# ScalarE takes two copies ahead of a square: a recurrence with a mixture of experts on one core

## The chip, the cores and the metric

The kernel runs on one core of a Trainium2 chip. Its five engines each work through a queue of their own in order: TensorE (PE, with its weight loads as PEld), VectorE (DVE), ScalarE (ACT), GpSimd (POOL) and SyncE (SP, which issues most transfers). The metric is the device time of one execution in microseconds, as the median of several runs. A profiled execution has its own time; its span runs from the first to the last instruction.

## The reference

Per batch and head, a 48 by 48 state decays and takes in one outer product per token; the result goes through a mixture of eight experts with one expert per token.

```python
for t in range(S):                                   # 4 batches, 8 heads, 768 tokens, 48 wide
    cur = np.einsum('bhd,bhe->bhde', u[None] * kt, vt)
    y[:, :, t] = np.einsum('bhd,bhde->bhe', rt, state + cur)
    state = w[None, :, :, None] * state + np.einsum('bhd,bhe->bhde', kt, vt)
...
logits = x @ w_gate + modality_bias[modality_id]     # x: 3072 x 384, 8 experts
e_idx = np.argmax(logits, axis=1)
gate_w = probs[np.arange(N), e_idx]
out[mask] = gate_w[mask, None] * (np.maximum(x[mask] @ w1[e], 0.0) @ w2[e])
```

## The kernel before

The first part works through 24 **units**: 6 chunks of 128 tokens by 4 batches, the batches innermost. A unit's result `x` (128 tokens by 384) is made in one PSUM bank `py`; what its tokens add to the state, and the eight numbers `d` per token that carry the `u` term, are made in a bank `pst`, of which there is one only (`ps_s` has one buffer): the matmuls of the next unit's `pst` can start when all readers of this one are done. There are two `py` banks, so `py` of unit i waits for the last reader of unit i-2.

The order on every engine is the order of the code: `run` is a hand-written schedule, and nothing reorders it. Step i of its loop works on several units at once:

- PE: turns f16 rows of unit i-2 (`raised`, tile `pxT`, units 6 to 11), turns keys of unit i+2 (`keys_turned`, `pkT`), scores of unit i+1 (`scores`, `psc`), then `values(i)`: `py` (lines 475 and 482), `pst` (491 and 496) and `bonus` (411), which leaves the eight columns of `d` of unit i+1 in `pst`.
- `token(i-1)`: DVE adds `dv` to `py` (504), ACT squares the sum for its norm (519), in place for the later scaling. `taken(i)`: DVE copies the eight columns `d` out of PSUM (419). `settled_state(i-1)` (units 4 to 13) or `state(i-1)` (units 0 to 3): ACT copies the new state out of `pst` in two halves (542, 534); from unit 14 on `state` is an add on DVE.
- `own(i)`: `dv = d v`, head by head on ACT (431); of units 9 to 13 (`SHARED`) GpSimd makes the second half in one instruction (427), at the end of its step's work.
- `factor`, `high`, `low`: two small DVE instructions make a power of two from the norm (314, 316), ACT writes the scaled f16 row (552) and DVE the f16 remainder (556). `raised` turns both on PE in the next step; `flipped` copies them out on ACT (580).
- GpSimd: `rk` for `bonus` (389), `rc` (364) three units ahead, `kt` (371) two ahead, and `send` (688), an indirect transfer of finished rows to DRAM.
- SP issues the loads; `pace` makes it wait for `d` of unit i (and for the norm's factor) before the next ones.

A group of 3 or 4 units is routed together (`logits`, `choose`, `count`, `place`): chains of small DVE instructions on 8 to 32 columns, one of which `fill()` slips in at each call. Their tables lie partly in a PSUM bank `pr`, partly in SBUF (`xinv`, `zs`, `pos`). `settle` (planned at step 8) and `ahead` make the numbers for jobs that run beside the units: with step 13 the first expert's weights are ready, and eight 128-row jobs (`s_up`, `s_high`, `s_low`, `s_down`) stand among the later units. Their weights are loaded in twelve pieces, normed on ACT (961, `norm`, steps 7 to 12) and split into f16 halves `whi` (ACT, 992) and `wlo` (DVE, 997); three `wlo` of step 13 are what the first job's `s_down` waits for. From about 200 us on a loop of expert jobs fills PE.

Of the kernel before, what the change touches and what calls it, by code (L numbers as in the profile page):

```python
# [9 lines left out]
F32 = mybir.dt.float32  # L10
# [5 lines left out]
ALU = mybir.AluOpType  # L16
# [31 lines left out]
TURNED = range(1, 15)  # L48
RAISED = range(6, 12)
OWNED = range(17, 24)  # L50

NE = 9
EARLY = 3
# [12 lines left out]
class _Kernel:  # L66
# [346 lines left out]
    def taken(self, i):  # L413
        u = self.ctx_[i]
        u["d"] = self.a.tile([P, H], F32, tag="d", name=f"d{i}", bufs=4)
        if i in OWNED:
            self.nc.vector.reduce_sum(u["d"], u["rk"].rearrange("p (h e) -> p h e", e=D), axis=AX.X)
            return
        self.nc.vector.tensor_copy(u["d"], u["pd"])  # L419

    def own(self, i, q):
        nc, u = self.nc, self.ctx_[i]
        if q == 0:
            u["dv"] = self.a.tile([P, DM], F32, tag="dv", name=f"dv{i}")
        if q and i in SHARED:
            half = lambda t: t[:, DM // 2 :].rearrange("p (h e) -> p h e", e=D)
            nc.gpsimd.tensor_mul(half(u["dv"]), half(u["v"]), u["d"][:, H // 2 :].unsqueeze(2).to_broadcast([P, H // 2, D]))
            return
        for h in range(q * H // 2, (q + 1) * H // 2):
            sl = slice(h * D, (h + 1) * D)  # L430
            nc.scalar.activation(u["dv"][:, sl], u["v"][:, sl], AF.Copy, scale=u["d"][:, h : h + 1])  # L431
# [160 lines left out]
    def choose(self, u):  # L592

        nc, a, n = self.nc, self.a, u["n"]
        lg, lo = u["lg"], u["lo"]
        gb = lambda ap: ap.unsqueeze(1).to_broadcast([P, n, E])
        eb = lambda ap: ap.unsqueeze(2).to_broadcast([P, n, E])
        new = lambda t, w=E, dt=F32: (a.tile([P, B, E], dt, tag=t, name=f"{t}{lo}")[:, :n, :] if w > 1 else a.tile([P, B], dt, tag=t, name=f"{t}{lo}")[:, :n])

        xinv = a.tile([P, B, 2], F32, tag="xinv", name=f"xinv{lo}")[:, :n, 0]  # L600
        nc.vector.tensor_scalar(xinv.bitcast(I32), u["sx"][:, :n].bitcast(I32), -1.0, float(254 << 23), ALU.mult, ALU.add)
        yield
        L = u["pr"][:, 320 : 320 + n * E].rearrange("p (g e) -> p g e", g=n)
        nc.vector.reduce_sum(L, lg.rearrange("p g w e -> p g e w"), axis=AX.X)
        yield
        nc.vector.scalar_tensor_tensor(L, L, self.wginv, eb(xinv), ALU.mult, ALU.mult)
        yield
        nc.vector.tensor_add(L, L, self.lb[:, lo : lo + n, :])
        yield
        mx = new("mx", 1)  # L610
        nc.vector.reduce_max(mx, L, axis=AX.X)
        yield
        bank = lambda c, w=E: u["pr"][:, c : c + n * w].rearrange("p (g w) -> p g w", g=n)
        d = bank(384)
        nc.vector.tensor_sub(d, L, eb(mx))
        yield
        er = bank(416)
        nc.vector.scalar_tensor_tensor(er, d, 0.0, gb(self.rev), ALU.is_equal, ALU.mult)
        ex = new("ex")
        nc.scalar.activation(ex, d, AF.Exp)  # L620
        yield
        mr = new("mr", 1)
        nc.vector.reduce_max(mr, er, axis=AX.X)
        yield
        u["oh"] = new("oh", dt=F16)
        nc.vector.tensor_tensor(u["oh"], er, eb(mr), ALU.is_equal)
        yield "oh"
        zs = new("zs", 1)
        nc.vector.reduce_sum(zs, ex, axis=AX.X)
        yield  # L630
        nc.vector.scalar_tensor_tensor(zs, zs, 1e-9, u["sx"][:, :n], ALU.add, ALU.mult)
        yield
        nc.vector.reciprocal(u["row"][:, :n, 2 * DM : 2 * DM + 2].bitcast(F32).rearrange("p b o -> p (b o)"), zs)
        yield
# [13 lines left out]
    def place(self, u):  # L648
# [6 lines left out]
        yield  # L655
        nc.vector.tensor_mul(v, v, u["oh"])
        yield
        pos = a.tile([P, B], F32, tag="pos", name=f"pos{lo}")[:, :n]
        nc.vector.reduce_sum(pos, v, axis=AX.X)
        yield  # L660
        u["posi"] = a.tile([P, B], I32, tag="posi", name=f"posi{lo}", bufs=3)
# [108 lines left out]
    def settle(self):  # L770

        nc, c = self.nc, self.c
        eid = self.eid0
        nc.vector.tensor_scalar_mul(self.ctl[:, E : 2 * E], eid, float(CAP))
        yield
        self.row0f = c.tile([1, 1], F32, name="row0f")
        nc.vector.tensor_scalar_mul(self.row0f, eid[:, 0:1], float(CAP))
        yield
        self.row0m = c.tile([1, 1], F32, name="row0m")
        yield  # L780
        nc.vector.tensor_scalar_add(self.row0m, self.row0f, -float(E * CAP + P))
        yield

    def ahead(self, ks, u=None):
# [364 lines left out]
    def run(self):  # L1149
# [99 lines left out]
        for i in range(NU - 1):  # L1249
# [13 lines left out]
            if down is not None:  # L1263
                self.s_high(down, 1)
                self.s_down(down, 0)
            if i == O + 5:
                self.settled_state(i - 1)
            self.token(i - 1) if i else None
            if ups.get(i - 2) is not None:
                self.s_take(ups[i - 2])  # L1270
            if i and i - 1 == self.grp["lo"]:
                groups[i - 1] = self.grp
            fill()
            each(i, self.taken) if i else None
            if i != O + 5:
                each(i - 1, self.settled_state)
            if i - 2 in RAISED:
                self.flipped(i - 2)
            if 0 < i < NU - 5:
# [1 line left out]
                each(i + 5, self.turned)  # L1281
            half(2 * (i - O) + 4)
            for j in range(2):
                each(i - 1, lambda i: self.state(i, j))
                fill()
            if down is not None:
                self.s_low(down, 1)
# [272 lines left out]
```

## Time and profile before

| | |
|---|---|
| median of 3 runs | 342.07 us (338.2 to 344.01) |
| profiled execution: time | 343.19 us |
| profiled execution: span | 341.3 us, granted TensorE clock 0.997 |
| busy: PE, PEld | 322.7 us (95%), 262.8 us (77%) |
| busy: DVE, ACT, POOL | 213.3 us (63%), 180.1 us (53%), 160.5 us (47%) |
| chain that ended last | 12 pieces, the last 3 us of the span |

The chain that ended last reaches back over the end alone, so it says nothing of the units. PE's busy share is the number to take apart by stretches: what is left of PE's time, and who ends its waits, is in the rows below.

### The profile page before, as it was taken

Reading aid. Unit: us, or ns where it says so; the run is one execution under the profiler, and the core shown is the slowest. Engines: PE = TensorE matmul, PEld = TensorE weight load, DVE = VectorE, ACT = ScalarE, POOL = GpSimd, SP = SyncE. Lnnn points to the kernel's source line nnn. Section 1 sums busy time; section 2 is a strip of 40 time slices with the busy share of each in tenths; the row PEclk is TensorE's granted clock in tenths of the full one; section 3 lists DMA queues with packets and bytes.
Section 4 is the critical chain, followed back from the end, with each engine's and each line's share of the span. In section 5 each row is a group of like instructions: output and inputs, shape, how many; then the busy total and the mean of one; then the engine's idle time right before and its main releaser. Section 6 shows DMA issues by size and latency. Waiting matters only on the chain. (4 is left out here: it accounts for less than half of the span.)

```text
span 341.3 us, 15249 instructions
## 1 busy us (share of the span) xinstructions
PE 322.7 (95%) x5459; PEld 262.8 (77%) x5459; DVE 213.3 (63%) x745; ACT 180.1 (53%) x482; POOL 160.5 (47%) x237
## 2 busy tenths in 40 slices
PE   7999998889899999899999999999999999999992
PEld 3788897778778888687887778886888887777771
DVE  7868987489997997587758732268322332334950
ACT  7787788578766568367532222265222224553820
POOL 8978779688739786526268411112122111211211
PEclk9999999999999999999999999999999999999998
DMA  6766999667659999995345632217611121112110
GB/s 187 237 165 161 169 250 301 181 224 169 182 139 234 195 281 285 235 131 147 71 130 175 190 96 65 47 46 249 195 46 46 47 69 23 46 52 64 37 46 5
DMA packets 58013, 47.93 MB, mean 140 GB/s; under 512 B 42344, under 2 KB 50807, under 8 KB 57712
## 3 DMA queue, kind: packets, MB, share of 16 engines
q1 hardware_dynamic: 54768, 37.85, 46.9%
q0 software_dynamic: 3200, 9.47, 7.7%
q8 instruction: 30, 0.49, 0.6%
q14 instruction: 15, 0.12, 0.1%
HBM read 27.21 MB, written 11.83 MB: 114 GB/s over the span
## 5 line engine op out<-in xcount | busy, mean ns | idle before, releaser
L1051 PEld LDWEIGHTS <-whi 128*128 128x128 f16 x1248 | 72.4, 98 | 3.8 <-issue 0.9
L1060 DVE SCALAR_TENSOR_TENSOR hl<-phb,hh 128x256 f16<-128x256 f32 (+1 forms) x48 | 24.4, 508 | 68.3 <-ACTq L1491 68.3
L1114 PEld LDWEIGHTS <-hh 128*128 128x128 f16 x416 | 39.1, 98 | 27.6 <-issue 2.2
L1051 PE MATMUL phb<-mxT,whi 128*128 128x128 f16 x768 | 50.8, 219 | 0.0
L431 ACT ACTIVATE dv<-kv,d 128x48 f32<-128x48 f32 x172 | 43.1, 325 | 0.4 <-DVE d L419 0.2
L1055 ACT ACTIVATE hh<-phb 128x256 f16<-128x256 f32 (+1 forms) x48 | 21.5, 455 | 32.6 <-PE phb L1051 21.9
L1051 PEld LDWEIGHTS <-wlo 128*128 128x128 f16 x624 | 37.7, 98 | 0.0
L1020 POOL TENSOR_TENSOR seenb<-otb,putb 128x1 int32<-128x1 int32 x16 | 4.4, 275 | 64.0 <-ACTq L1491 51.9
L451 DVE TENSOR_TENSOR at<-psc,mask 128x512 f32<-128x512 f32 x48 | 31.9, 682 | 1.9 <-PE psc L445 1.8
L364 POOL TENSOR_TENSOR rc<-ud,powr 112x512 f32<-112x512 f32 (+1 forms) x25 | 31.0, 1243 | 0.7 <-DMA ud<-in_pd 0.5
L1114 PEld LDWEIGHTS <-hl 128*128 128x128 f16 x208 | 19.4, 98 | 15.3 <-issue 2.5
L1011 ACT ACTIVATE otb<-po,fac 128x384 f32<-128x384 f32 x16 | 9.3, 580 | 39.5 <-PE phb L1051 36.1
L688 POOL DMA_INDIRECT rows<-row,posi x24 | 25.0, 1042 | 10.8 <-DVE base L664 3.1
L445 PE MATMUL psc<-rc,kc 64*64 64x128 f32 (+1 forms) x768 | 27.1, 276 | 2.3 <-issue 1.5
L1051 PE MATMUL phb<-mxT,wlo 128*128 128x128 f16 x384 | 29.3, 219 | 0.0
L1114 PE MATMUL po<-whi,hl 128*128 128x384 f16 x136 | 28.0, 326 | 1.2 <-PEq L1556 0.7
L1114 PE MATMUL po<-whi,hh 128*128 128x384 f16 x136 | 27.7, 326 | 0.5 <-ACT hh L1055 0.4
L1114 PE MATMUL po<-wlo,hh 128*128 128x384 f16 x136 | 27.6, 326 | 0.0
L1051 PE MATMUL phs<-mxT,whi 128*128 128x128 f16 x432 | 27.2, 219 | 0.0
L445 PEld LDWEIGHTS psc<-rc,kc 64*64 64x64 f32 (+1 forms) x768 | 20.9, 132 | 7.9 <-issue 4.2
L482 PE MATMUL py<-kv,at 128*64 128x48 f32 x768 | 26.5, 221 | 0.0
L997 DVE SCALAR_TENSOR_TENSOR wlo<-raw,ws,whi 128x1024 f16<-128x1024 f32 (+1 forms) x20 | 25.0, 1277 | 1.4 <-issue 0.6
(287 smaller groups left out, 636.0 us busy)
## 6 DMA issues: line engine op xcount, KB each, us to landing
kv<-in_pt SPq DMA_DIRECT2D x21, 384.0 KB
ud<-in_pd SPq DMA_DIRECT2D x10, 384.0 KB
raw<-in_w SPq DMA_DIRECT2D x12, 256.0 KB
raw<-in_w SPq DMA_DIRECT2D x6, 512.0 KB
raw<-in_w SPq DMA_DIRECT2D x2, 1536.0 KB, 6.3
ud<-in_pd SPq DMA_DIRECT2D x14, 192.0 KB
rows<-pad SPq DMA_DIRECT2D x10, 193.0 KB
rt<-in_pt SPq DMA_DIRECT2D x7, 192.0 KB
```

The source lines that it names most:

```text
L364: nc.gpsimd.tensor_mul(u["rc"][:TOP, s], u["rT"][:TOP, s], self.powr[:TOP, s])
L431: nc.scalar.activation(u["dv"][:, sl], u["v"][:, sl], AF.Copy, scale=u["d"][:, h : h + 1])
L445: nc.tensor.matmul(u["ps"][j][s, pr * P : (pr + 1) * P], u["kc"][r, pr, s], u["rc"][r, pr, :], start=True, stop=True)
L451: nc.vector.tensor_mul(u["at"][:, j * NPR : (j + 1) * NPR, :], u["ps"][j].rearrange("p (q t) -> p q t", q=NPR), self.mask.unsqueeze(1).to_ ...
L482: nc.tensor.matmul(py[t, sl], u["at"][:, j * NPR + pr, t], u["v"][:, sl], start=c == h == 0, stop=h == H - 1, skip_group_check=True)
L688: i = nc.gpsimd.indirect_dma_start(out=self.rows, out_offset=bass.IndirectOffsetOnAxis(ap=u["posi"][:, b : b + 1], axis=0), in_=u["row"][: ...
L997: self.nc.vector.scalar_tensor_tensor(self.wlo[:, sl], self.raw[:, sl], sc, self.whi[:, sl], ALU.mult, ALU.subtract)
L1011: self.nc.scalar.activation(ot, po[:, :DM], AF.Copy, scale=gf[:, t : t + 1])
L1051: self.nc.tensor.matmul(ph[:, q * P : (q + 1) * P], w[:, c0 : c0 + P], self.xT[:, xq, t * P : (t + 1) * P], start=i == q == 0, stop=i == l ...
L1055: self.nc.scalar.activation(self.hh[:, f0 : f0 + fb, t * P : (t + 1) * P], p3, AF.Relu)
L1060: self.nc.vector.scalar_tensor_tensor(self.hl[:, f0 : f0 + fb, r], p3, 0.0, self.hh[:, f0 : f0 + fb, r], ALU.max, ALU.subtract)
L1114: self.nc.tensor.matmul(po[:, :DM], h[:, f, t * P : (t + 1) * P], w[:, c0 : c0 + DM], start=first, stop=last)
```

## The change

Four edits. (1) In steps 1 to 12 `taken(i)` is a copy on ACT, and ACT's queue gets the state copies of unit i-1 and then `d` of unit i ahead of the square of unit i-1; at step 13 and later `d` stays on DVE, and at steps 13 and 14 the state copies alone go ahead of the square. (2) GpSimd's half of `dv` is issued right behind `taken`. (3) Three numbers of `settle` are made on ACT in place of DVE. (4) `xinv`, `zs` and `pos` move into the PSUM bank `pr`; the summed logits go to an SBUF tile `lgs`.

```diff
+EASED = 13
...
-        self.nc.vector.tensor_copy(u["d"], u["pd"])
+        (self.nc.scalar.copy if i < EASED else self.nc.vector.tensor_copy)(u["d"], u["pd"])
+
+    def shared(self, i):
+        if i in SHARED:
+            u = self.ctx_[i]
+            u["dv"] = self.a.tile([P, DM], F32, tag="dv", name=f"dv{i}")
+            half = lambda t: t[:, DM // 2 :].rearrange("p (h e) -> p h e", e=D)
+            self.nc.gpsimd.tensor_mul(half(u["dv"]), half(u["v"]), u["d"][:, H // 2 :].unsqueeze(2).to_broadcast([P, H // 2, D]))
...
-        if q == 0:
+        if q == 0 and i not in SHARED:
             u["dv"] = self.a.tile([P, DM], F32, tag="dv", name=f"dv{i}")
         if q and i in SHARED:
-            half = lambda t: t[:, DM // 2 :].rearrange("p (h e) -> p h e", e=D)
-            nc.gpsimd.tensor_mul(half(u["dv"]), half(u["v"]), u["d"][:, H // 2 :].unsqueeze(2).to_broadcast([P, H // 2, D]))
             return
...
-        xinv = a.tile([P, B, 2], F32, tag="xinv", name=f"xinv{lo}")[:, :n, 0]
+        xinv = col(448)
...
-        nc.vector.reduce_sum(L, lg.rearrange("p g w e -> p g e w"), axis=AX.X)
+        raw = new("lgs")
+        nc.vector.reduce_sum(raw, lg.rearrange("p g w e -> p g e w"), axis=AX.X)
...
-        zs = new("zs", 1)
+        zs = col(456)
...
-        pos = a.tile([P, B], F32, tag="pos", name=f"pos{lo}")[:, :n]
+        pos = pr[:, 452 : 452 + n]
...
-        nc.vector.tensor_scalar_mul(self.ctl[:, E : 2 * E], eid, float(CAP))
+        nc.scalar.activation(self.ctl[:, E : 2 * E], eid, AF.Copy, scale=float(CAP))
...
-        nc.vector.tensor_scalar_mul(self.row0f, eid[:, 0:1], float(CAP))
+        nc.scalar.activation(self.row0f, eid[:, 0:1], AF.Copy, scale=float(CAP))
...
-        nc.vector.tensor_scalar_add(self.row0m, self.row0f, -float(E * CAP + P))
+        nc.scalar.activation(self.row0m, self.row0f, AF.Copy, bias=-float(E * CAP + P))
...
-            if i == O + 5:
-                self.settled_state(i - 1)
+            each(i - 1, self.settled_state)
+            if 0 < i <= B:
+                self.state(i - 1, 0)
+                self.state(i - 1, 1)
+            if i and i < EASED:
+                self.taken(i)
+                self.shared(i)
             self.token(i - 1) if i else None
...
             fill()
-            each(i, self.taken) if i else None
-            if i != O + 5:
-                each(i - 1, self.settled_state)
+            if i >= EASED:
+                self.taken(i)
+                self.shared(i)
...
             for j in range(2):
-                each(i - 1, lambda i: self.state(i, j))
+                if i > B:
+                    self.state(i - 1, j)
                 fill()
```

In three places the order on an engine is what the prediction speaks of. The first is ACT in steps 4 and 5 (the number behind a name counts tiles: `py_665` and `pst_682` are unit 3's, `py_779` and `pst_804` unit 4's). Before:

```order
L519 ACTIVATE row_402,ssq_404<-py_665 128x384
L534 COPY st_99<-pst_682 64x4x48
L726 ACTIVATE rev_728<-idxf 128x8
L727 ACTIVATE rev_728<-idxf 128x8
L534 COPY st_99<-pst_682 48x4x48
L730 COPY n_727<-pswg 128x1
L431 ACTIVATE dv_760<-kv_93,d_733 128x48 x4
L552 ACTIVATE row_402<-py_665,sx_405 128x384
L431 ACTIVATE dv_760<-kv_93,d_733 128x48 x4
L519 ACTIVATE row_856,ssq_858<-py_779 128x384
L542 COPY st_98<-pst_804 64x4x48
L542 COPY st_98<-pst_804 48x4x48
```

And of the changed kernel, the end of the same place:

```order
L730 COPY n_731<-pswg 128x1
L437 ACTIVATE dv_760<-kv_93,d_727 128x48 x4
L558 ACTIVATE row_406<-py_665,sx_409 128x384
L437 ACTIVATE dv_760<-kv_93,d_727 128x48 x4
L548 COPY st_98<-pst_804 64x4x48
L548 COPY st_98<-pst_804 48x4x48
L420 COPY d_857<-pst_804 128x8
L525 ACTIVATE row_860,ssq_862<-py_779 128x384
```

The state copies and `d` stand ahead of the square that waits for DVE's add; the square went from third last to last.

The second is ACT in step 9, the one step to which `settle` also moves its instructions (`junk` is `norm` of a piece of the weights). Before:

```order
L961 ACTIVATE junk,wssq<-raw 128x1024
L519 ACTIVATE row_1420,ssq_1422<-py_1333 128x384
L542 COPY st_99<-pst_1358 64x4x48
L542 COPY st_99<-pst_1358 48x4x48
L580 COPY xT_857<-pxT_1387 128x768
L431 ACTIVATE dv_1462<-kv_93,d_1426 128x48 x4
L552 ACTIVATE row_1420<-py_1333,sx_1423 128x384
L961 ACTIVATE junk,wssq<-raw 128x1024
```

Now:

```order
L968 ACTIVATE junk,wssq<-raw 128x1024
L548 COPY st_99<-pst_1356 64x4x48
L548 COPY st_99<-pst_1356 48x4x48
L420 COPY d_1419<-pst_1356 128x8
L525 ACTIVATE row_1424,ssq_1426<-py_1331 128x384
L782 ACTIVATE ctl<-eid_879 1x8
L586 COPY xT_861<-pxT_1385 128x768
L785 ACTIVATE row0f<-eid_879 1x1
L788 ACTIVATE row0m<-row0f 1x1
L437 ACTIVATE dv_1421<-kv_93,d_1419 128x48 x4
L558 ACTIVATE row_1424<-py_1331,sx_1427 128x384
L968 ACTIVATE junk,wssq<-raw 128x1024
```

Four instructions more stand between the first norm and the second.

The third is GpSimd in steps 13 and 14, beside which DVE's three `wlo` stand. Before:

```order
L389 TENSOR_TENSOR rk_2013<-rc_1747,kc_1905 112x512
L688 DMA rows<-row_856,posi_1909 25856x772
L364 TENSOR_TENSOR rc_2071<-ud_85,powr 112x512
L688 DMA rows<-row_856,posi_1909 25856x772
L371 TENSOR_TENSOR kt_97<-kv_89,wtok 128x4x96
L427 TENSOR_TENSOR dv_2088<-kv_92,d_2061 128x192
L389 TENSOR_TENSOR rk_2265<-rc_1902,kc_2075 112x512
L688 DMA rows<-row_856,posi_1909 25856x772
L364 TENSOR_TENSOR rc_2303<-ud_86,powr 112x512
L688 DMA rows<-row_856,posi_1909 25856x772
L371 TENSOR_TENSOR kt_94<-kv_90,wtok 128x4x96
```

Now:

```order
L390 TENSOR_TENSOR rk_2009<-rc_1749,kc_1903 112x512
L427 TENSOR_TENSOR dv_2059<-kv_92,d_2057 128x192
L696 DMA rows<-row_860,posi_1907 25856x772
L365 TENSOR_TENSOR rc_2069<-ud_85,powr 112x512
L696 DMA rows<-row_860,posi_1907 25856x772
L372 TENSOR_TENSOR kt_97<-kv_89,wtok 128x4x96
L390 TENSOR_TENSOR rk_2261<-rc_1900,kc_2073 112x512
L696 DMA rows<-row_860,posi_1907 25856x772
L365 TENSOR_TENSOR rc_2299<-ud_86,powr 112x512
L696 DMA rows<-row_860,posi_1907 25856x772
L372 TENSOR_TENSOR kt_94<-kv_90,wtok 128x4x96
```

`dv` of unit 13, which needs `d` of that unit, stands ahead of two sends, `rc` and `kt` that need nothing of it.

## Rows read from the trace of the kernel before

**Rows 1.** Busy time by stretch: us, then PE, PEld, DVE, ACT, POOL, clock, DMA

```profile
27.00:100.00 73.00, 65.68 (x1658) 57.90 (x1656) 61.08 (x201) 53.84 (x160) 53.78 (x53) 1.00 0.77 196
100.00:200.00 100.00, 98.61 (x1727) 81.64 (x1726) 74.14 (x285) 53.09 (x161) 59.25 (x95) 1.00 0.79 187
```

**Rows 2.** Who waited for whom, PE, 20 to 100 us: total, times, longest

```profile
PE py L475 <- issue: 1.7, 1, 1.7
PE psc L445 <- issue: 1.5, 1, 1.5
PE pos L1114 <- DVE wlo L997: 1.4, 2, 0.7
PE pxT L565 <- DVE row L556: 1.4, 3, 0.6
...
PE pxT L565 <- ACT row L552: 0.4, 1, 0.4
PE pst L491 <- ACT st L542: 0.2, 1, 0.2
```

**Rows 3.** The same view, PE, from 100 us to the end

```profile
PE pst L496 <- issue: 1.3, 1, 1.3
```

**Rows 4.** The same view, PE's weight loads, 20 to 40 us

```profile
PEld py L475 <- DVE row L556: 0.4, 1, 0.4
...
PEld pst L491 <- ACT st L542: 0.3, 1, 0.3
...
PEld pst L491 <- ACT st L534: 0.2, 1, 0.2
```

**Rows 5.** Timeline of ACT, 28.9 to 36 us: start, us, what, idle before

```profile
30.12 0.32 ACT L534 COPY st<-pst 48x192 f32<-48x192 f32 x1
30.46 0.16 ACT L730 COPY n<-pswg 128x1 f32<-128x1 f32 x1
...
34.64 0.49 ACT L519 ACTIVATE row<-py 128x384 f16<-128x384 f32 x1 [1.47 <-DVE py L504]
...
35.12 0.63 ACT L542 COPY st<-pst 64x192 f32<-64x192 f32 x2
```

**Rows 6.** Who waited for whom, ACT, 27 to 84 us

```profile
ACT row L519 <- DVE py L504: 7.0, 8, 1.5
```

**Rows 7.** Timeline of ACT, 75.9 to 81 us

```profile
77.15 0.49 ACT L519 ACTIVATE row<-py 128x384 f16<-128x384 f32 x1 [0.84 <-DVE py L504]
...
79.89 0.56 ACT L552 ACTIVATE row<-py,sx 128x384 f16<-128x384 f32 x1
```

**Rows 8.** Timeline of ACT, 52.5 to 60 us

```profile
54.56 1.06 ACT L961 ACTIVATE junk<-raw 128x1024 f16<-128x1024 f32 x1 [1.04 <-DMA raw<-in_w]
```

**Rows 9.** Timeline of DVE, five places between 39 and 93 us

```profile
39.18 0.97 DVE L601 TENSOR_SCALAR xinv<-sx 128x4 int32<-128x4 int32 x1
...
60.82 0.20 DVE L601 TENSOR_SCALAR xinv<-sx 128x4 int32<-128x4 int32 x1
...
69.07 1.26 DVE L997 SCALAR_TENSOR_TENSOR wlo<-raw,ws,whi 128x1024 f16<-128x1024 f32 x1
...
83.78 0.14 DVE L419 COPY d<-pst 128x8 f32<-128x8 f32 x1
...
90.32 2.82 DVE L997 SCALAR_TENSOR_TENSOR wlo<-raw,ws,whi 128x1024 f16<-128x1024 f32 x1
```

**Rows 10.** Timeline of POOL, 38 to 99 us

```profile
39.38 0.73 POOL L274 MEMSET pad<- 128x772 int16 x1
...
77.45 0.51 POOL L427 TENSOR_TENSOR dv<-kv,d 128x192 f32<-128x192 f32 x1 [1.89 <-DVE pr L656]
...
89.99 1.01 POOL L688 DMA_INDIRECT rows<-row,posi  x1 [0.17 <-issue]
91.04 1.01 POOL L371 TENSOR_TENSOR kt<-kv,wtok 128x384 f32<-128x384 f32 x1
98.12 1.27 POOL L389 TENSOR_TENSOR rk<-rc,kc 112x512 f32<-112x512 f32 x1 [6.08 <-DVE pr L608]
```

More of the change, by code (lines that the diff above doesn't have):

```diff
@@ L598, in choose @@
         new = lambda t, w=E, dt=F32: (a.tile([P, B, E], dt, tag=t, name=f"{t}{lo}")[:, :n, :] if w > 1 else a.tile([P, B], dt, tag=t, name=f"{t}{lo}")[:, :n])
-        xinv = a.tile([P, B, 2], F32, tag="xinv", name=f"xinv{lo}")[:, :n, 0]
+        bank = lambda c, w=E: u["pr"][:, c : c + n * w].rearrange("p (g w) -> p g w", g=n)
+        col = lambda c: u["pr"][:, c : c + n]
+        xinv = col(448)
         nc.vector.tensor_scalar(xinv.bitcast(I32), u["sx"][:, :n].bitcast(I32), -1.0, float(254 << 23), ALU.mult, ALU.add)
@@ L603, in choose @@
         L = u["pr"][:, 320 : 320 + n * E].rearrange("p (g e) -> p g e", g=n)
-        nc.vector.reduce_sum(L, lg.rearrange("p g w e -> p g e w"), axis=AX.X)
+        raw = new("lgs")
+        nc.vector.reduce_sum(raw, lg.rearrange("p g w e -> p g e w"), axis=AX.X)
         yield
-        nc.vector.scalar_tensor_tensor(L, L, self.wginv, eb(xinv), ALU.mult, ALU.mult)
+        nc.vector.scalar_tensor_tensor(L, raw, self.wginv, eb(xinv), ALU.mult, ALU.mult)
         yield
@@ L612, in choose @@
         yield
-        bank = lambda c, w=E: u["pr"][:, c : c + n * w].rearrange("p (g w) -> p g w", g=n)
         d = bank(384)
@@ L773, in settle @@
         eid = self.eid0
-        nc.vector.tensor_scalar_mul(self.ctl[:, E : 2 * E], eid, float(CAP))
+        nc.scalar.activation(self.ctl[:, E : 2 * E], eid, AF.Copy, scale=float(CAP))
         yield
         self.row0f = c.tile([1, 1], F32, name="row0f")
-        nc.vector.tensor_scalar_mul(self.row0f, eid[:, 0:1], float(CAP))
+        nc.scalar.activation(self.row0f, eid[:, 0:1], AF.Copy, scale=float(CAP))
         yield
         self.row0m = c.tile([1, 1], F32, name="row0m")
-        yield
-        nc.vector.tensor_scalar_add(self.row0m, self.row0f, -float(E * CAP + P))
+        nc.scalar.activation(self.row0m, self.row0f, AF.Copy, bias=-float(E * CAP + P))
         yield
```

## Prediction

> **What bounds the kernel now.** I read the page first for shares, and its chain only to set it aside: it covers the last microseconds. Then the stretches: from 100 us on PE is busy 98.61 of 100 us, so nothing that another engine does there comes out of the time [rows 1]. What can be won lies before: from 27 to 100 us PE is busy 65.68 of 73.00, so 7.3 us are idle. Third, who ends PE's waits there [rows 2]. Two lines make up 3.2 us (1.7 and 1.5) with no engine named: they stand in the middle of a group of matmuls that waits for nothing, and one more of 1.3 us stands past 100 us [rows 3]. The change doesn't touch them: PE's own order is the same row for row. The rest are waits for others: 1.4 us for the `wlo` of step 13, 1.4 + 0.4 us for the f16 rows that `raised` turns, 0.2 us for a state copy. So at most some 3.4 us of 342 are within reach of any edit on ACT, DVE and GpSimd in these steps, and the change reaches a part.
>
> **The change part by part.**
>
> *State and `d` ahead of the square.* ACT sits idle before the square 7.0 us in 8 waits between 27 and 84 us [rows 6], because the add on DVE isn't done; the two state copies behind it take 0.63 us [rows 5], and need nothing of that add. Now they fill the idle time, and the square's own time is unchanged where the wait was longer. Three places where PE feels it:
>
> 1. Step 4. The second state copy ended at 30.44 after two `rev` of `first_order` had gone between [rows 5]; the weight load of `pst` waited 0.2 us for it [rows 4]. The same lateness made `n` start at 30.46, DVE's chain behind `n` late, and with it the remainder row that holds the `py` bank: 0.4 us [rows 4].
> 2. Step 5. The copies ran at 35.12, behind a square that had waited 1.47 us; `pst` waited 0.3 us (weight loads) or 0.2 us (matmuls) for their end [rows 2, 4, 5]. They can now run from 33.2, where ACT fell idle (34.64 less 1.47).
>    The weight loads give 0.2 + 0.4 + 0.3 = 0.9 us, the matmuls alone show 0.2 us. Matmuls overlap, so a stop shorter than one of them is hidden in PE's row; the truth is nearer to the weight loads: I take **-0.7** (0.2 to 0.9).
> 3. Step 12. ACT waits 0.84 us before the square at 77.15 [rows 7]; the copies (0.63) and `d` fit in, and `high` at 79.89 [rows 7] comes about 0.6 us sooner. PE's wait for `high` is 0.4 us, the one for `low` behind it some 0.4 of the 1.4, the mean of the two shorter of three [rows 2]; 0.3 of these 0.8 I leave, since `low` also stands behind DVE's own work. In steps 10 and 11 the remainder row hangs on DVE's own order, which isn't shorter: nothing there. **-0.5** (0 to 0.7; 1.8 if all `pxT` waits went).
>
> *Its price on ACT.* `d` has no row on ACT; the nearest is `n`, a PSUM column to SBUF, 0.16 us [rows 5], so 0.05 (it overlaps its neighbours) to 0.2 us a step in 12 steps. Where ACT waits anyway (8 of these) it is free. In step 9 it isn't: a norm waited for a load until 54.56 [rows 8], and all that is behind it, up to the next norm, runs without a pause. There `d` and three instructions of `settle` come in, 4 x 0.16 = 0.6 us, at most 0.8: the norm that PE's small matmul for the scale waits for, and the f16 row of unit 8, come that much later. What covers it is PE's own stop of 1.7 us just there, in `py` of step 9 [rows 2]; I take **0**, and +0.8 if that stop is gone.
>
> *Tables in PSUM, `settle` on ACT.* `xinv` took 0.97 us at 39.18, beside a GpSimd memset, and 0.20 at 60.82 [rows 9, 10]: such a small instruction can stand still until GpSimd's is done. The edit takes 0.8 us out of DVE in step 6, and 16 instructions in all leave its queue. But PE names no wait for DVE in step 6, so it is worth **0** (0 to -0.3), and a reduction into SBUF in place of PSUM costs nothing that a row shows. The Trainium skill, "SBUF — State Buffer", section "Who interferes with whom", says why: copies and `tensor_scalar` from SBUF to SBUF can take the port pair shared with GpSimd, and the loser waits for the whole instruction; the trace agrees with that for `xinv` (0.97 against 0.20 us). No term hangs on it.
>
> *GpSimd's half sooner.* No row has DVE's add wait for GpSimd's `dv`, so the earlier half wins nothing by itself. What it adds is a wait with a queue behind it: `dv` at 77.45 already waited 1.89 us for `d` with nothing but `rk` behind [rows 10]; now it waits with two sends, `rc` and `kt` behind. These have two steps of slack (their matmuls come two units later), so PE doesn't wait for them. But they move in time, and what they move into is the three `wlo` of step 13. Before, the first of them took 2.82 us against 1.26 for one alone: a send at 89.99 and `kt` at 91.04, which ended at 92.05, ran first; then GpSimd had nothing until 98.12 [rows 9, 10]. PE's 1.4 us [rows 2] are the price of this 1.56 us. With `dv` of unit 13 waiting for `d`, which is there at 83.9 [rows 9], `dv` 0.5, send 1.2 with its pause, `rc` (of `rk`'s shape) 1.3, send 1.2, `kt` 1.0 and `rk` 1.3 [rows 10] end near 90.4, and a send, `rc`, a send and `kt` are still to come, up to 95. So the first `wlo` either slips in behind `rk` (-1.5 us) or waits as before, and the other two may now meet a GpSimd instruction each (about +1.1 us each, at most 1.3). I take **0**, bounds -1.5 to +1.9.
>
> The Trainium skill's rule of the same section would let a `wlo` wait for one GpSimd instruction in progress and no more, because the one that comes first holds the ports for its whole length. The row speaks against it: 2.82 us is the wait for a send and for `kt` behind it. By the rule the first `wlo` would lose at most 1.3 us where it lost 1.56, and the sum would be 0.3 us lower, 340.6.
>
> **The sum.** -0.7 - 0.5 = -1.2 us. Against the profiled execution's own 343.19 us (span 341.3 and 1.9 around it) that is 342.0. This execution lies 1.1 us above the median of the three runs, and the sum carries over: 342.07 - 1.2 = **340.9 us**. A measurement of this kernel can tell about 2% (6.8 us) from no change; this is a third of a per cent.
>
> **The rivals.**
>
> *A. The deferred GpSimd work meets the `wlo` (slower).* For it: GpSimd is free from 92.05 to 98.12 now and would be busy to 95; against it: DVE's next `wlo` stands ready as soon as the one before ends, so GpSimd may be the one that waits, as in 1.26 us for the `wlo` at 69.07 [rows 9]. It decides from two further collisions on: +1.9 - 1.2, and with step 9's +0.8 up to +1.5: 342.8 to 343.6, slightly slower than before.
>
> *B. The first `wlo` slips in between (faster).* -1.5 more: 339.4. The order of `rk` and the send near 90.4 against a `wlo` due at 90.32 decides by tenths.
>
> *C. PE loses elsewhere what it gains.* PE comes 0.7 us sooner to step 9, where the norm waits for a load that lands when it lands (54.56), so the gain of steps 4 and 5 ends there, as waiting for `pxT`, and step 12 alone stays or not: -0.5 to 0, 341.6 to 342.1.
>
> **How the numbers follow.** Forecast 0.45, C 0.2, A 0.18, B 0.17. What none of them fixes are PE's stops without a named cause, 1.7, 1.5 and 1.3 us in this execution: one more or fewer is +-1.5, and the runs before spread from 338.2 to 344.0. The range runs from B with one stop fewer (339.4 - 1.5, and 0.7 for pxT waits: 337.2) to A with half a stop more (343.6 + 0.8 = 344.4): 337.2 to 344.4. Two per cent faster would be 335.2, below the sum of every wait in reach (342.07 - 3.4 = 338.7) with two stops gone: 0.03. Two per cent slower, 348.9, needs A with three stops more: 0.03. Within 2%: 0.94.
>
> **What would show it.** Right: no PE wait for `st` or the `py` bank between 28 and 37 us, the wait before the square moved behind `d`, `high` of unit 11 sooner and the two waits near 80.5 us gone, `xinv` at 0.2 us everywhere. GpSimd's `dv` with waits of 2 us or more before it, and `rc` and `kt` some 3 us later in steps 11 to 14. The three `wlo` of step 13 decide between forecast, A and B: 2.8 us for the first and 1.3 for the others, or two long ones, or none. Wrong: PE's idle time from 27 to 100 us the same or larger apart from the stops without a cause, or more PE waits for DVE's rows in steps 9 to 12 than 1.8 us.

## The result, and the profile after

| | before | after |
|---|---|---|
| median (22 runs each) | 340.39 us | 343.1 us |
| lowest to highest | 338.2 to 344.01 us | 340.11 to 347.33 us |
| ratio after / before | | 1.0061, 95% interval 1.0038 to 1.0083 |
| the same, measured a second time (35 and 12 runs) | 340.01 us | 342.01 us, ratio 1.0018 (0.9979 to 1.0057) |

The medians take in every run; the ratios leave out runs more than 1.5% above the fastest of their kernel, and the first profiled execution below is one of these.

The difference is within the 2% that such a measurement can tell with certainty. In the first series the sign is plain all the same: 2.1 us slower by the ratio, 2.7 by the medians, where 1.2 us faster was forecast. In the second series the interval takes in no change. The first profiled execution of the changed kernel is the longest of its 22 (347.33 us, span 345.3); a profiled execution of the second series took 341.98 us (span 340.0), and both are read below.

First the windows of the long execution, as in [rows 1], and then three short ones inside the first (start and end, length, busy us of PE, PEld, DVE, ACT, POOL, granted clock, DMA):

```profile
27.00:100.00 73.00, 62.68 (x1565) 56.58 (x1564) 55.52 (x169) 51.94 (x159) 51.24 (x51) 0.95 0.75 185
100.00:200.00 100.00, 99.11 (x1758) 81.54 (x1756) 77.63 (x299) 54.14 (x166) 60.00 (x95) 1.00 0.78 190
...
68.00:73.60 5.60, 5.19 (x141) 4.65 (x139) 5.57 (x6) 1.93 (x6) 5.57 (x7) 1.00 0.85 241
73.60:78.50 4.90, 0.08 (x3) 0.00 (x0) 3.76 (x15) 3.65 (x10) 1.78 (x2) 0.96 0.16 39
78.10:84.90 6.80, 6.34 (x93) 5.67 (x95) 6.35 (x21) 6.54 (x16) 4.02 (x5) 0.50 0.79 217
```

From 100 us on PE is as busy as before. Before that, PE is busy 62.68 us where it was 65.68 [rows 1]. It stands for nearly 5 us from 73.6 on, and from 78.1 on, near the end of that stop, the granted clock is 0.50, the lower of its two levels (1.2 GHz of 2.4), for 6.8 us: 93 matmuls in 6.34 busy us there, against 155 in 6.13 in the same stretch of before. At most half of the 6.8 us is lost that way, so stop and clock together are worth up to 8 us in this execution, more than the whole difference of the medians.

Who waited for whom, PE, 20 to 100 us, to be set beside [rows 2]:

```profile
PE pr L650 <- DVE row L641: 4.9, 1, 4.9
PE py L488 <- issue: 2.8, 2, 1.4
PE psc L451 <- issue: 0.8, 1, 0.8
PE pos L1121 <- DVE wlo L1004: 0.7, 1, 0.7
PE pst L502 <- issue: 0.6, 1, 0.6
PE pxT L571 <- DVE row L562: 0.4, 1, 0.4
```

What the forecast meant to remove is removed: no `pst` waits for an ACT state copy, and of 1.8 us for f16 rows 0.4 are left. New are 4.9 us for a DVE reciprocal (`row`, 641) ahead of `count`'s matmuls of group 1. Why DVE was so late stands in its timeline from 68.8 us (start, us, what, idle before in brackets):

```profile
68.87 0.19 DVE L620 TENSOR_REDUCE mx<-pr 128x4 f32<-128x32 f32 x1
68.98 5.09 DVE L1004 SCALAR_TENSOR_TENSOR wlo<-raw,ws,whi 128x1024 f16<-128x1024 f32 x1
73.99 0.55 DVE L510 TENSOR_TENSOR py<-py,dv 128x384 f32<-128x384 f32 x1
...
78.33 0.18 DVE L641 RECIPROCAL row<-pr 128x4 f32<-128x4 f32 x1
```

One `wlo` took 5.09 us; in before the same one, of step 10, took 1.26 [rows 9]. Unit 10's add stands behind it, then the square, the routing's exponential, and the reciprocal. GpSimd over the same time:

```profile
57.15 0.51 POOL L427 TENSOR_TENSOR dv<-kv,d 128x192 f32<-128x192 f32 x1 [4.36 <-ACT d L420]
58.01 1.17 POOL L696 DMA_INDIRECT rows<-row,posi  x1 [0.35 <-POOL dv L427]
...
68.10 1.01 POOL L372 TENSOR_TENSOR kt<-kv,wtok 128x384 f32<-128x384 f32 x1
69.05 1.28 POOL L390 TENSOR_TENSOR rk<-rc,kc 112x512 f32<-112x512 f32 x1
70.28 0.52 POOL L427 TENSOR_TENSOR dv<-kv,d 128x192 f32<-128x192 f32 x1
70.74 1.28 POOL L365 TENSOR_TENSOR rc<-ud,powr 112x512 f32<-112x512 f32 x1
71.98 1.00 POOL L372 TENSOR_TENSOR kt<-kv,wtok 128x384 f32<-128x384 f32 x1
72.92 1.19 POOL L678 COPY row<-tok 128x4 int32<-128x4 int32 x1
```

Read them together: GpSimd's five instructions from `kt` to `kt` run head to tail, 68.10 to 72.98, and `wlo` comes through only behind the last. It ends at 74.07, so its own 1.27 us began near 72.8, and the small copy of `row`, 0.19 us in before, stretches to 1.19 beside it: now GpSimd is the one that waits. The queue is this long because `dv` of unit 9 waited 4.36 us for `d`, with two sends, `rc` and `kt` behind it; in before GpSimd stood idle for 3.01 us ahead of this step's `rk`. The three `wlo` of step 13, where the prediction looked, took 1.99, 1.27 and 2.02 us (2.82, 1.27, 1.27 in before), together no more than there.

In the second execution the same `wlo` began during `rk`, slipped in when GpSimd stood idle for 0.32 us, and took 1.83 us. The waits of PE there, 20 to 100 us:

```profile
PE pr L650 <- DVE row L641: 1.6, 1, 1.6
PE pos L1121 <- DVE wlo L1004: 1.4, 2, 0.7
PE psc L451 <- issue: 1.0, 1, 1.0
PE pst L502 <- issue: 0.8, 1, 0.8
```

And two windows of that execution, with the granted clock third from the end:

```profile
38.20:41.50 3.30, 3.30 (x46) 2.62 (x46) 1.95 (x9) 1.93 (x7) 2.27 (x5) 0.50 1.23 203
75.70:79.00 3.30, 3.30 (x46) 2.63 (x45) 3.23 (x11) 3.04 (x12) 2.13 (x3) 0.50 0.68 181
```

So 5.09 us is not what every execution pays, but a stop of 1.6 us at the same place and a fall of the clock behind it are there again. From 27 to 100 us PE is busy 66.86 us in this execution, more than the 65.68 of before: what it loses there it loses at the lower clock.

### The profile page after: what moved, and what is told of

It reads as the page before. It is cut to its first block, busy times and chain, and to the rows that moved or that the text cites. A ratio compares the mean times of both kernels' runs of the same rounds, so it can differ in the third digit from the quotient of the medians.

```text
span 345.3 us, 15244 instructions
## 1 busy us (share of the span) xinstructions
PE 324.9 (94%) x5459; PEld 265.2 (77%) x5459; DVE 212.0 (61%) x729; ACT 181.3 (53%) x498; POOL 160.0 (46%) x237
## 5 line engine op out<-in xcount | busy, mean ns | idle before, releaser
L488 PE MATMUL py<-kv,at 128*64 128x48 f32 x768 | 27.4, 224 | 2.8 <-issue 2.8
L451 PE MATMUL psc<-rc,kc 64*64 64x128 f32 (+1 forms) x768 | 28.0, 282 | 1.7 <-POOL rc L365 1.0
L1004 DVE SCALAR_TENSOR_TENSOR wlo<-raw,ws,whi 128x1024 f16<-128x1024 f32 (+1 forms) x20 | 28.3, 1437 | 1.4 <-issue 0.7
L488 PEld LDWEIGHTS py<-kv,at 128*64 128x64 f32 x768 | 25.8, 141 | 3.7 <-issue 3.5
L451 PEld LDWEIGHTS psc<-rc,kc 64*64 64x64 f32 (+1 forms) x768 | 21.6, 136 | 7.8 <-issue 3.1
```

What stands on the lines that cost most here:

```text
L451: nc.tensor.matmul(u["ps"][j][s, pr * P : (pr + 1) * P], u["kc"][r, pr, s], u["rc"][r, pr, :], start=True, stop=True)
L488: nc.tensor.matmul(py[t, sl], u["at"][:, j * NPR + pr, t], u["v"][:, sl], start=c == h == 0, stop=h == H - 1, skip_group_check=True)
L1004: self.nc.vector.scalar_tensor_tensor(self.wlo[:, sl], self.raw[:, sl], sc, self.whi[:, sl], ALU.mult, ALU.subtract)
```

## The experiments

Four theories stood at the start. **1**: GpSimd's half of `dv`, issued sooner, delays GpSimd, and DVE's `wlo` pays. **2**: `zs` in the bank `pr` makes `count` wait for the reciprocal. **3**: ACT's extra instructions cost in step 9. **4**: the reorder's gain is taken back by PE's own stops and by the clock. The kernels ran on several chips, so each is compared with runs of the kernel before beside it. Every kernel here does the whole computation.

### Which edit costs: four kernels

**e1_own_place**, the changed kernel with GpSimd's half back at its old place:

```diff
     def shared(self, i):
...
-            half = lambda t: t[:, DM // 2 :].rearrange("p (h e) -> p h e", e=D)
-            self.nc.gpsimd.tensor_mul(half(u["dv"]), half(u["v"]), ...)
...
     def own(self, i, q):
...
         if q and i in SHARED:
+            half = lambda t: t[:, DM // 2 :].rearrange("p (h e) -> p h e", e=D)
+            nc.gpsimd.tensor_mul(half(u["dv"]), half(u["v"]), ...)
             return
```

> The changed kernel with one edit undone: GpSimd's half of dv is issued at its old place, at the end of the step's work, and everything else stays changed. Theory 1 (GpSimd): dv issued sooner waits 4.4 us for d in step 9, pushes two sends back, and the wlo of step 10 at 69 us then stands still for 3.8 us behind kt, rk, dv, rc, kt of GpSimd. Without it the wlo of step 10 takes 1.3 to 2.3 us, PE's 4.9 us wait ahead of count falls below 0.5, and the time is 3 to 5 us under the changed kernel's profiled one, 339 to 340.5 as a median. Theory 2 (the bank): count waits for the reciprocal because zs lies in the bank pr; then a PE wait of over 1.5 us for the reciprocal stays and the time is that of the changed kernel, 342 to 343.5. Theory 3 (ACT's extra work): also 342 to 343.5, with PE's waits on f16 rows in steps 9 to 12.

344.23 us against 344.14, ratio 1.0003 (0.9967 to 1.0039). The loss is gone, as theory 1 has it; the gain of 1.2 us isn't there either. A wait of 1.8 us for the reciprocal stays, as theory 2 has it, without making this kernel slow.

**e2_zs_sbuf**, the changed kernel with one table back:

```diff
-        zs = col(456)
+        zs = new("zs", 1)
```

> The changed kernel with zs back in an SBUF tile; all else stays changed. Theory 1 (GpSimd): the wlo of step 10 still takes 4 to 5 us, PE still stands 3 us or more there, now until oh or the f16 row, and the time is within 1 us of the changed kernel, 342 to 343.5. Theory 2 (the bank): PE's wait for the reciprocal is gone and the time is 340 to 341; the wlo may still be long.

346.94 against 344.14, ratio 1.0056 (1.0018 to 1.0095): as slow as the changed kernel, with no wait for the reciprocal at all. Theory 2 falls as a price. But theory 1's long `wlo` is not in this execution either. On DVE, step 10:

```profile
71.03 1.28 DVE L1004 SCALAR_TENSOR_TENSOR wlo<-raw,ws,whi 128x1024 f16<-128x1024 f32 x1
```

What stands there is lower clock, 3.4 us from 41.0 and 6.8 us from 64.9.

**e3_sooner_only**, the kernel before with GpSimd's half sooner alone:

```diff
+    def shared(self, i):
...
-            each(i, self.taken) if i else None
+            each(i, self.taken, self.shared) if i else None
```

> The kernel before with one edit: GpSimd's half of dv is issued right behind the copy of d, which stays on DVE at its old place. Theory 1 in its simple form (any sooner issue packs GpSimd's queue): a wlo of 3 us or more in steps 10 to 13 and 1.5 to 3 us above the kernel before. Theory 1 with ACT (d has to sit on ACT behind the norms for the delay): dv waits under 2.5 us in step 9, no wlo over 2.9 us, and the time within 0.7 us of the kernel before. Theories 2 and 3: no difference from the kernel before.

346.0 against 344.14, ratio 1.0050 (1.0021 to 1.0078). The sooner half alone costs about 1.7 us by the ratio. Neither form of theory 1 has this trace right: the `wlo` of step 10 took 1.34 us, because here `dv` waits for a `d` that stands on DVE behind that very `wlo`, and GpSimd is idle meanwhile. DVE and GpSimd in step 10:

```profile
67.08 1.34 DVE L1002 SCALAR_TENSOR_TENSOR wlo<-raw,ws,whi 128x1024 f16<-128x1024 f32 x1
...
68.92 0.15 DVE L419 COPY d<-pst 128x8 f32<-128x8 f32 x1
...
69.21 0.51 POOL L426 TENSOR_TENSOR dv<-kv,d 128x192 f32<-128x192 f32 x1 [1.87 <-DVE d L419]
```

The three `wlo` of step 13 took 2.42, 1.27 and 2.02 us, and PE's wait for an f16 row in step 11 was 1.2 us, with 3.4 us of lower clock at it. So that the edit costs is shown here, but not that it costs through the `wlo` of step 10.

**e4_reorder_only** and, in a later series, **e9_reorder_again**: the kernel before with the order on ACT alone.

```diff
...
+            each(i - 1, self.settled_state)
+            if 0 < i <= B:
+                self.state(i - 1, 0)
+                self.state(i - 1, 1)
+            if i and i < EASED:
+                self.taken(i)             # d as a copy on ACT
             self.token(i - 1) if i else None
...
```

> The kernel before with one edit: state copies and d on ACT ahead of the square in steps 1 to 12 (state copies alone in 13 and 14). Nothing else: GpSimd's half of dv at its old place, settle on DVE, tables where they were. By the prediction's terms -0.7 -0.5, so about 1.2 us below the kernel before, 339.2 with 340.4 as its median. Theory 3 (ACT's extra work in step 9 costs): 0.5 to 1.5 us above the kernel before, 341 to 342, with PE waiting for ACT near 55 to 60 us. Theories 1 and 2 say nothing here but that no wlo takes over 2.9 us.

> The kernel before with the reorder on ACT alone, as measured once already (344.01 against 344.14), for a second estimate. By the prediction's sum -1.2 us. By theory 4 (the gain of steps 4 and 5 is taken back by PE's own stops near 37 us and by stretches of half clock): within 0.7 us of the kernel before, a stop of 0.3 to 0.9 us in the pst group of step 5 where the kernel before has none of its size, a mean granted clock of 0.991 or less where the kernel before has 0.993.

344.01 against 344.14, ratio 0.9957 (0.9915 to 0.9998), and 342.6 against 343.48, ratio 0.9966 (0.9941 to 0.9992): by the ratios 1.2 to 1.5 us faster, by the medians 0.1 and 0.9; both intervals end just below 1. The forecast's sum for this edit holds, and theory 3 falls.

### The same again, and where the sooner half costs

**b2_before** is the kernel before, unchanged, for a second profile; **a2_after** is the changed kernel, whose rows stand above.

> The kernel before, unchanged, profiled once more beside the others. All theories: the time of the kernel before. Wanted from it: the times of the units' first score matmuls and the stretches of half clock, to set beside the other kernels on the same chip. By the granted clocks so far (0.994 in the mean of 35 runs) no stretch of half clock, or one of 3.4 us, before the end.

> The changed kernel, unchanged, on the same chip as the others. If the 5.1 us wlo of step 10 is what the change costs in every execution, it stands here again (4 us or more) and the time is 2 to 3 us above the kernel before. If that was one collision of many possible ones, the time is again 2 to 3 us above, the wlo of step 10 may be 1.3 us, and the stretches of half clock (two of 3.4 us by the mean granted clock of 0.986) stand behind other PE stops.

The kernel before again took 340.38 us against 340.01, with PE stops of 1.2 us at 61.6 and up to 0.6 us at `pxT`, and no stretch of lower clock before the end. The changed kernel took 342.01 us against 340.01, and 5.09 us did not come again (1.83): the second possibility named for it, one collision of many possible ones.

**e5_sooner_11_12**, **e7_sooner_9_10_13** and **e8_sooner_9_10** are the changed kernel with the sooner half in some units only:

```diff
     def shared(self, i):
-        if i in SHARED:
+        if i in SOONER:                   # (11, 12), (9, 10, 13), (9, 10)
...
```

> The changed kernel with GpSimd's half of dv sooner in units 11 and 12 alone, the two steps with no send behind it; in units 9, 10 and 13 it is at its old place. Theory 1 as it stands (dv waits for d with the sends behind it, and these then meet DVE): the loss is gone, within 0.7 us of the kernel with dv at its own place, so -0.7 to +0.8 against the kernel before. Rival (any sooner dv costs, by packing rk and dv against wlo in every step): +0.8 to +1.5 against the kernel before.

> The complement of the kernel with units 11 and 12: the changed kernel with GpSimd's half sooner in units 9, 10 and 13 alone, the three steps in which sends stand behind it. Theory 1 (the cost lies where sends are held back): the whole loss, +1.5 to +2.8 us against the kernel before, two of the three wlo of step 13 with a collision of 0.7 us or more, mean granted clock 0.986 to 0.989. Rival (the loss is spread over all five): +0.6 to +1.4.

> The changed kernel with GpSimd's half sooner in units 9 and 10 alone; 11 to 13 at their old place. If the loss comes from steps 9 and 10 (dv waits there for a d that stands behind a norm on ACT, two sends come late, and the wlo of step 10 meets a packed GpSimd): +1.3 to +2.5 us against the kernel before. If it comes from step 13 (two of the three wlo meet an instruction where one did): -0.5 to +0.7, and the first of those wlo is clean as in the kernels with dv at its own place.

Units 11 and 12: 340.15 against 340.01, ratio 1.0013 (0.9983 to 1.0043). Units 9, 10 and 13: 347.54 against 343.48, ratio 1.0111 (1.0088 to 1.0133). Units 9 and 10: 348.83 against 343.48, ratio 1.0144 (1.0114 to 1.0175). The price lies in the two steps with sends ahead of the `wlo` of step 10, and not in step 13. It is twice what was expected, and more than with all five units sooner (e2, on the same chip: 1.0056), so units 11 and 12 seem to give some of it back when they are sooner too; how wasn't found. The kernel with units 9 and 10, its timeline of all engines near the `wlo` of step 10, DVE and GpSimd:

```profile
69.49 1.27 POOL L366 TENSOR_TENSOR rc<-ud,powr 112x512 f32<-112x512 f32 x1
...
69.65 3.15 DVE L1008 SCALAR_TENSOR_TENSOR wlo<-raw,ws,whi 128x1024 f16<-128x1024 f32 x1
...
70.71 1.00 POOL L373 TENSOR_TENSOR kt<-kv,wtok 128x384 f32<-128x384 f32 x1
...
71.67 1.17 POOL L682 COPY row<-tok 128x4 int32<-128x4 int32 x1
```

It is the picture of the first profile, one size smaller: `wlo` waits through `rc` and `kt`, comes in ahead of the small copy, and PE then stops for 2.5 us ahead of `count`, again for the reciprocal. In the kernel with 13 as well that `wlo` took 3.69 us and the stop 3.3. Both show two stretches of 3.4 us at half clock.

**e13_wlo_moved** takes that `wlo` away from step 10, without touching GpSimd; **e14_reorder_moved** does the same to the kernel with the order on ACT alone.

```diff
-            plan(O + 2 + q, split(q))
+            if q:
+                plan(O + 2 + q, split(q))
+            else:
+                plan(O + 2, lambda: self.wide(0))     # whi, on ACT, where it was
+                plan(O + 4, lambda: self.fine(0))     # wlo, on DVE, two steps later
```

> The kernel with GpSimd's half sooner in units 9 and 10 (+5.3 us against the kernel before), with the first wlo moved from step 10 to step 12, where two stand now; the same work. Theory 1 (the price is DVE's wlo standing still behind GpSimd, and PE's count behind that): DVE has no instruction over 2.2 us in step 10, PE's stop ahead of count in step 11 falls from 2.5 us to under 1.2, and the time comes down by 2 to 4 us, to +1 to +3 against the kernel before. Rival (the price is GpSimd's own work, rk, rc and kt, coming late for PE and DVE): no change, +4 to +5.5.

> The control: the reorder on ACT alone (-0.9 and so far -0.1 us in the medians) with the same wlo moved from step 10 to step 12. If moving it is good in itself, this is 1 us or more below the reorder alone, -2 or less; if it only removes the collision that the sooner half makes, -0.3 to -1.5, as the reorder alone.

The first: 344.75 against 343.22, ratio 1.0037 (1.0006 to 1.0068), where it was 1.0144. The control: 342.78 against 343.22, ratio 0.9991 (0.9958 to 1.0025): moving it is no gain in itself. PE's waits in the first, 20 to 100 us:

```profile
PE pxT L575 <- DVE row L566: 0.3, 1, 0.3
...
PE pr L654 <- DVE row L645: 0.2, 1, 0.2
```

The 2.5 us ahead of `count` became 0.2, and no stretch of lower clock was left in that execution, although GpSimd's `kt`, `rk`, `rc` and `kt` still run head to tail there, 65.63 to 70.06 us. For the kernel with units 9 and 10 this settles the main cause: the sooner half costs through the `wlo` of step 10. By the ratio 1.3 us remain, some of which the move itself may cost: the control lies 0.3% above the reorder alone, within the intervals. For the changed kernel, with all five units sooner, the same cause is likely but not shown: its `wlo` of step 10 took 5.09 and 1.83 us in two executions, and e2 and e3, whose `wlo` was clean, lose 1.9 and 1.7 us.

### Where the reorder's own gain went

**e6_zs_own** is the changed kernel with GpSimd's half at its own place and `zs` in SBUF. **e10_state_only** is the kernel before with the state copies alone ahead of the square, `d` on DVE.

> The changed kernel with two things undone: GpSimd's half of dv at its own place, and zs back in SBUF. What stays: the order on ACT, settle on ACT, xinv and pos in the bank pr, the summed logits in SBUF. Theory 2 as a smaller term (the bank pr makes count wait for the reciprocal, 1.8 us at 74.0 in the kernel with dv at its own place): that wait is gone, 0.8 to 1.8 us less than there, so 0.7 to 1.7 us below the kernel before. Rival (that wait was cover for others that follow, oh or the f16 row): the PE stop stays under another name or moves to the three wlo, and the time is within 0.6 us of the kernel before.

> The kernel before with only the state copies ahead of the square; d stays on DVE at its old place, settle on DVE, tables where they were, GpSimd's half at its old place. By the prediction's sum -0.7 (steps 4 and 5) and -0.3 to -0.5 (step 12), about -1.1. By theory 4: within 0.7 us of the kernel before, with the same stop near 37 us as the kernel that moves d too. If d on ACT costs something in step 9 (theory 3), this one is 0.5 us or more below that kernel.

The first: 340.58 against 340.01, ratio 1.0008 (0.9972 to 1.0045); its rival is right: the 1.8 us that PE waited for the reciprocal in e1 it now waits for f16 rows (1.8 us in 2 waits, where e1 has 0.9 in one). The second: 342.42 against 343.48, ratio 0.9957 (0.9926 to 0.9988), as the reorder with `d`: `d` on ACT costs nothing, and gains nothing. Of theory 4 the stop near 37 us is there (0.5 us in e9, 0.9 in e10, where before has at most 0.2), but it doesn't take the gain back, and the mean granted clock of both (0.993 and 0.994) is that of the kernel before. So the order on ACT wins, and something in `settle` or the tables takes it back in e1 and e6.

**e11_reorder_settle** is the reorder with `settle` on ACT, **e12_reorder_tables** the reorder with `xinv` and `pos` in the bank and the summed logits in SBUF.

> The reorder on ACT and settle's three numbers on ACT; the tables as in the kernel before, GpSimd's half at its old place. If settle on ACT takes back the reorder's gain (three more instructions on ACT in step 8 or 9, where ACT has no pause, so that d and the f16 row come later): within 0.5 us of the kernel before. If the tables do: -0.7 to -1.5 us, as the reorder alone.

> The reorder on ACT and the tables (xinv and pos in the bank pr, summed logits in SBUF; zs stays in SBUF); settle on DVE, GpSimd's half at its old place. If the tables take back the reorder's gain (with xinv's 0.95 us gone at 38 us, DVE comes 0.1 us later or sooner to the wlo of step 10 than GpSimd to kt, and loses 0.7 us there): within 0.5 us of the kernel before and a wlo of 1.9 to 2.0 us in step 10. If settle does: -0.7 to -1.5 us, and that wlo takes 1.3 us.

344.66 against 343.22, ratio 1.0010 (0.9973 to 1.0048), and 342.75 against 343.22, ratio 0.9947 (0.9909 to 0.9985). This points to `settle`: the two intervals overlap a little, but e1 and e6, which have that edit too, show no gain either, while e4, e9 and e10, which don't, do. The timeline of all engines in e11, DVE and GpSimd at the `wlo` of step 10:

```profile
65.41 0.19 DVE L612 TENSOR_REDUCE mx<-pr 128x4 f32<-128x32 f32 x1
65.42 1.01 POOL L372 TENSOR_TENSOR kt<-kv,wtok 128x384 f32<-128x384 f32 x1
...
65.51 2.00 DVE L997 SCALAR_TENSOR_TENSOR wlo<-raw,ws,whi 128x1024 f16<-128x1024 f32 x1
```

`wlo` reaches DVE 0.09 us after GpSimd's `kt` has begun, and waits for it. In before it was 0.05 us ahead (69.07 in [rows 9]), and `kt` took 2.08 us instead of 1:

```profile
69.12 2.08 POOL L371 TENSOR_TENSOR kt<-kv,wtok 128x384 f32<-128x384 f32 x1
```

What turned the order is not ACT's work: the edit of `settle` also drops a `yield`, so every later small DVE instruction of the chains comes one call of `fill` sooner, and `mx` stands ahead of `wlo` where `skip` and `wlo` came first. **e15_settle_yield** puts the `yield` back into e11, **e16_all_yield** into e6:

```diff
         self.row0m = c.tile([1, 1], F32, name="row0m")
+        yield
         nc.scalar.activation(self.row0m, self.row0f, AF.Copy, bias=-float(E * CAP + P))
```

> The reorder and settle on ACT, with the yield put back between settle's second and third number, so that DVE's order at the first wlo is again that of the kernel before. If the order on DVE was the price: that wlo takes 1.3 us (1.99 without the yield) while GpSimd's kt takes 2.1, the PE stop in step 11 falls from 1.4 to 0.4 to 0.8 us, and the time is 0.7 to 1.5 us below the kernel before. If the work on ACT was the price: the wlo may be 1.3 us, but the time is within 0.5 us of the kernel before or above it.

> All edits but GpSimd's sooner half and zs in the bank, with the yield put back. If the order on DVE was the price that the kernel without the yield (+0.6 us) paid: -0.7 to -1.8 us against the kernel before, and xinv never over 0.3 us. If not: within 0.6 us of the kernel before.

339.84 against 340.61, ratio 0.9975 (0.9943 to 1.0006), and 339.94 against 340.61, ratio 0.9964 (0.9930 to 0.9997). The same place in e15:

```profile
68.13 0.14 DVE L820 TENSOR_SCALAR skip<-again 128x1 int32<-128x1 f32 x1
...
68.19 1.26 DVE L998 SCALAR_TENSOR_TENSOR wlo<-raw,ws,whi 128x1024 f16<-128x1024 f32 x1
...
68.25 2.07 POOL L372 TENSOR_TENSOR kt<-kv,wtok 128x384 f32<-128x384 f32 x1
```

0.06 us ahead of `kt`, `wlo` takes 1.26 us and GpSimd pays, which has time. PE's longest wait for an f16 row is 0.7 us, where e11 has 1.4. The intervals of e11 and e15 overlap, and so do those of e6 and e16 (1.0008 and 0.9964), so the times alone don't prove it; both pairs and the rows point the same way. Kernels with the `yield` and GpSimd's half at its old place have this `wlo` at 1.26 us (before twice, e4, e9, e10, e12, e15, e16), those without it at 1.99 to 2.00 (e1, e6, e11), but for e5 with 1.28. e16, and e12 with `settle` left on DVE, lie 1.2 and 1.8 us below the kernel before, with intervals that end just below 1.

## Why the prediction was wrong

- **The failed step is "GpSimd's half sooner"**, taken as 0 with bounds -1.5 to +1.9. Alone it cost 0.5%, 1.7 us (e3); by e1 against the changed kernel (1.0003 and 1.0061) 0.6%, 2.0 us; in units 9 and 10 alone 1.4%. So it lay at its upper bound, where the sum has 0; with what `settle`'s edit took back (below), that turns the forecast's -1.2 us into a loss. What failed in it is the sentence "what they move into is the three `wlo` of step 13". The deferred work begins in step 9, and the first `wlo` that it meets is the one of step 10; the row for it, 69.07, was on the page [rows 9] and served only as the price of an undisturbed one. That GpSimd's `kt` began 0.05 us behind it wasn't looked at.
- **The unit price was wrong too**: "may now meet a GpSimd instruction each (about +1.1 us each, at most 1.3)". A `wlo` that meets a full queue can wait through several instructions: 3.8 us for five. The Trainium skill, "SBUF — State Buffer", section "Who interferes with whom", says that an operation with two SBUF inputs contends with a GpSimd instruction that reads SBUF; that agrees with 5.09 against 1.26 us. The prediction had itself set the 2.82 us of [rows 9], a wait for two instructions, against the reading that only one is waited for, and yet priced each further collision as one.
- **Rival A had the sign and the kind of collision**, with the wrong place. It was to decide from two further collisions in step 13; these came (1.99 and 2.02 us), but the three `wlo` took 5.13 us from first start to last end, 5.21 in before, and PE waited no longer for them (1.4 us in all, as in [rows 2]). That 343.1 us lies in A's 342.8 to 343.6, and in the stated range, is luck in part: the sum starts from the 342.07 us of three runs, and 22 runs give 340.39, so the loss by the medians is 2.7 us, where A has 0.7 to 1.5.
- **"Worth 0" for `settle`** was the second error: "16 instructions in all leave its queue" counts work and not order. By e6 against e16 and e11 against e15 the lost `yield` cost some 1.2 to 1.5 us, an estimate from overlapping intervals, and as much as the reorder won.
- **State and `d` ahead of the square, -0.7 and -0.5: right in sum.** The waits named are gone in e9 and e10, and the order on ACT alone measured ratios of 0.9957, 0.9966 and 0.9957, so -1.2 to -1.5 us; how the gain divides between steps 4, 5 and 12 wasn't measured. Rival C, by which little of it would stay, isn't borne out. The price on ACT in step 9 was rightly 0: e9 and e10 can't be told apart.
- **Tables in PSUM: right in time, though not in the reason.** `xinv` takes 0.17 us at 38.42 in the changed kernel, as said. But the prediction looked for PE waits in step 6 alone, and `count` got a new one later, of 1.8 us in e1. Where it was taken out, the f16 row behind it came as late (e6), so it showed no price.
- **Not foreseen at all was the clock**: its mean over the runs was 0.986 and 0.989 for the changed kernel, 0.985 and 0.988 for e8 and e7, against 0.993 to 0.994 for the kernel before in every series. A stretch of 3.4 us at half clock is 0.005 of that mean, so by it the changed kernel has about one more of them per execution, each worth at most 1.7 us. Part of the prices above is theirs. They aren't the sooner half's alone: a stretch that begins between 38 and 42 us stands in eight of the profiled executions, all with the order on ACT and five of them with GpSimd's half at its old place, and e6, which loses no time, has a mean of 0.990.

Open stay three things: why the sooner half in units 11 and 12 makes up for part of what it costs in 9 and 10; where the 1.3 to 1.9 us lie of kernels with a sooner half and a clean `wlo` in step 10 (e2, e3, e13), whose traces show other collisions and the clock, no single one; and whether the long wait in step 10 needs the lost `yield` besides. The three kernels that show this `wlo` at over 3 us (the changed one, e7, e8) have the sooner half, `d` on ACT and no `yield`; one with the first two and the `yield` put back wasn't run.

## What to carry to other kernels

An instruction that is issued sooner and then waits moves everything queued behind it: follow that queue to the first place where it meets another engine, not to the place where the trouble was last seen. Where two engines' long instructions start within 0.1 us of each other in the trace, name which one yields: an edit elsewhere may turn it, as the lost `yield` did here. Where generators interleave instructions, count the yields that an edit adds or drops, since they set the order of all that follows.

## What the runs showed of the hardware

- A DVE `wlo` (two SBUF inputs, 1.26 us alone) that starts after a GpSimd instruction can wait through a chain of them: 2.00 us behind one `kt`, 3.15 behind `rc` and `kt`, 5.09 behind five. It doesn't always: in e7 the `wlo` of step 11 started during `rc`, took 1.57 us and came in ahead of the `kt` that follows head to tail, which then took 1.99 us. Which of the two will happen the rows don't say.

```profile
75.59 1.28 POOL L366 TENSOR_TENSOR rc<-ud,powr 112x512 f32<-112x512 f32 x1
...
76.38 1.57 DVE L1008 SCALAR_TENSOR_TENSOR wlo<-raw,ws,whi 128x1024 f16<-128x1024 f32 x1
76.82 1.99 POOL L373 TENSOR_TENSOR kt<-kv,wtok 128x384 f32<-128x384 f32 x1
```

- Where `wlo` starts first by 0.05 us (before) or 0.06 (e15), GpSimd waits instead (`kt` 2.08 and 2.07 us for 1.0). But 0.03 us were not enough in e4 (`wlo` at 82.07, 2.41 us, GpSimd's `rc` at 82.10), nor 0.06 in e3 (`wlo` at 89.82, 2.42 us, `rc` at 89.88). So at such distances the order of the starts in a trace doesn't decide who waits.
- The granted clock fell to half for 3.4 us, or 6.8: 1.5 us after the end of a PE stop of 0.8 us (at 38.1), 0.8 us after one of 1.6 us (at 75.7), and near the end of one of 4.9 us (at 78.1). It stayed at 1.00 behind stops of 1.7 and 1.5 us in before [rows 2]. So in these rows a stop's length alone doesn't say whether the clock falls.
